# Turning LayerNorm's output by transposing DMAs of float16 halves instead of by TensorE

## The chip, the cores and the metric

The kernel runs on one core of one Trainium2 chip. A core has five engines that each run their own instructions in order: TensorE (PE, matrix products; its weight loads are shown apart as PEld), VectorE (DVE), ScalarE (ACT), GpSimd (POOL) and SyncE (SP), which here issues nearly all DMAs. The metric is the device time of one execution in microseconds (us), smaller is better, as the median over runs.

## The reference

The inputs are x of 2048 rows and 512 columns in float32, and the weights of an attention block and of a gated MLP. Cut to what matters:

```python
def _layernorm(x, axis=-1, eps=1e-5):
    m = jnp.mean(x, axis=axis, keepdims=True)
    v = jnp.var(x, axis=axis, keepdims=True)
    return (x - m) / jnp.sqrt(v + eps)

def attention(x, wqkv, wo):          # 32 heads of 16
    q, k, v = split(x @ wqkv)
    p = softmax(q @ k.T * 16 ** -0.5)
    return (p @ v) @ wo

def gated(x, w_in, w_sp, b_sp, w_out):   # w_in: 512 x 1376, w_sp: 2048 x 2048
    z = gelu(x @ w_in)
    z1, z2 = z[..., :688], layernorm(z[..., 688:])
    g = w_sp @ z2 + b_sp[:, None]
    return (z1 * g) @ w_out

h = x + attention(_layernorm(x), wqkv, wo)
out = h + gated(_layernorm(h), w_in, w_sp, b_sp, w_out)
```

## The kernel before

**Arithmetic.** Float32 products are made of float16 parts: an operand is split into `hi`, its float16 rounding, and `lo`, the float16 rounding of what is left. `mm3` (lines 107 to 109) makes three matmuls: hi by hi, hi by lo, lo by hi, all into one PSUM tile in float32.

**Stages.** The rows are worked in 16 blocks of 128. The prologue (0 to about 160 us) normalizes x block by block, turns each block so that the 512 columns lie on the partitions (four pieces of 128x128 side by side), and makes v, q and k of it; the attention stage (to about 1293 us) does the 32 heads and prepares the spatial products; the z stage (to about 1452 us) makes h, LN(h), gelu of its product with `w_in` and the LayerNorm of its second half, block by block; a last stage makes the spatial products and the output.

**How a block is turned.** The normalized block is float32 in SBUF. TensorE's `transpose` with an identity matrix turns one piece of 128x128 into PSUM, four to a block, into a tile `tp` (L424 in the prologue's `turn_only`, L1177 in the z stage's `turn`). Then ACT copies `tp` to a float16 tile (`hi`: L433, L98), and DVE subtracts that from `tp` for `lo` (L431, L104). The results are `xT` in the prologue and `hT` in the z stage.

**Order.** Around both places the order is written out by hand, under a manual schedule for all five engines: each engine does its instructions in the order of the program text, and waits where an operand or a buffer is not ready. A tile with `bufs=2` has two buffers; its third use waits until the first is read. SP issues the DMAs in text order too, and they are spread over eight lanes in turn: a DMA waits for the one eight places before it.

**The prologue's groups.** Blocks 4 to 15 go through a loop over g = 0, 1, 2, with a = 4g the blocks whose v is made by `proj(proj_v, ...)` and b = 4g + 4 the blocks that are normalized meanwhile. `stats` and `scales` (DVE) give mean and scale of four blocks at once, ending in `nb` (L401); `normal` (ACT, L412) normalizes one block in place (tile `xg`); `turn_x` turns blocks. `proj_qk` makes k and q of 512 rows, whose float16 parts `part` (ACT L458, DVE L461) go out to `k_scr` and `q_scr`; `kf` are two more copies by ACT of k for the maxima of the softmax (L472, L473), and v goes out to `v_scr`. PSUM has three tiles `acc` for these products, used in turn. In group 2 `load_wqk(1)` loads the next weights for q and k (`wg`, L345, on SP); `weigh_wqk(1)` takes their largest entries on DVE (`most`, L352) and spreads them on POOL (`each`, L356); `measure` is a small product of it on PE (`m`, L374), which stands in PE's order behind `proj_v(12)`.

**The z stage's loop.** Per block k, PE does `make_h` of block k + 2 (L747, 12 matmuls), then four products of 12 matmuls, `make_z`, of block k, with the transposes of block k + 1 between them. ACT does `split_o` of block k + 3 (tile `o`, L737, its `lo` on DVE L740), the four gelus of block k (L1192), `hT`, then `hn`, the normalized h of block k + 2 (L1271), and the normalization of z (L1214) with float16 copies of it (`b`, L1196). DVE does for each block: `o`, `hT`, the chain from `mv` (L758) to `nb` (L768) for LN(h) of block k + 2, in every second block a part `b` that was put off (L1197), the statistics of z (`zst`, L1265), the chain from `zmv` (L1211) to `nb`, then h itself (`xr`, L751) and its statistics. SP loads the attention's output `o` and the reciprocal row sums `rc` of block k + 5 (four DMAs each, L723 and L726) once `o`'s buffer is free; POOL multiplies the two (L731).

Of the kernel before, what the change touches and what calls it, by code (L numbers as in the profile page):

```python
# [59 lines left out]
def block_kernel(ctx: ExitStack, tc: tile.TileContext, x, wqkv, wo, w_in, w_sp4, b_sp, w_out, out):  # L60
# [208 lines left out]
    with ExitStack() as pre:  # L269
# [6 lines left out]

        xT = [pc.tile([P, DB, S], F16, name=f"xT{i}") for i in range(2)]
        wv = [pc.tile([P, DB, D], F16, name=f"wv{i}") for i in range(2)]
# [147 lines left out]
        def put_x(sb, *which):  # L426

            c = slice(sb * P, (sb + 1) * P)
            for i in which:
                if i:  # L430
                    nc.vector.tensor_sub(xT[1][:, :, c], tps[sb], xT[0][:, :, c])  # L431
                else:
                    nc.scalar.activation(xT[0][:, :, c], tps[sb], AF.Copy)  # L433

        def turn_x(*blocks):

            for sb in blocks:
                turn_only(sb)
                put_x(sb, 0, 1)
# [172 lines left out]
        for g in range(3):  # L612
            a, b = 4 * g, 4 * g + 4
            mv = moments(4)
            if g:
                proj(proj_v, a)
                turn_x(a + 2, a + 3)
                if g == 1:
# [6 lines left out]
                normal = scales(mv)  # L625
                normal(b, b + 1)
                proj(proj_v, a + 3)
# [14 lines left out]
            if g == 2:  # L642
                load_wqk(1)
            proj(proj_qk, 0, g, 0, then=lambda: turn_x(b, b + 1), at=1 if g else 2)
            if not g:
                load_x(12)
                load_x(13)
            normal(b + 2, b + 3)
        weigh_wqk(1)
        proj(proj_v, 12)  # L650
        turn_x(14, 15)
        load_wqk(2)
# [62 lines left out]
    h_rows = [0, 1, HB, HB + 1] + [sb + HB * i for sb in range(2, HB) for i in range(2)]  # L715
    os_, o2s, xrs, hns, hTs = {}, {}, {}, {}, {}

# [43 lines left out]
    def new_hn(sb):  # L761
        mv, rs = scale_h(sb)
        hns[sb] = e2.tile([P, D], F32, name="hn", bufs=3)
        nc.vector.tensor_scalar(hns[sb], xrs.pop(sb), mv[:, 0:1], rs, op0=ALU.subtract, op1=ALU.mult)

    def minus_mean(pool, mv, rs):
# [21 lines left out]
    with ExitStack() as at:  # L788
# [256 lines left out]
        for n in range(0, len(units), 2):  # L1045
# [94 lines left out]
            if n == 502:  # L1140
                new_hn(h_rows[0])
        weigh(*prev)
        take(*prev[:2], e2)
# [22 lines left out]
    with ExitStack() as mid:  # L1166
        m2 = mid.enter_context(tc.tile_pool(name="mid_2", bufs=2))
        zs, zst = {}, {}
        ps = mid.enter_context(tc.tile_pool(name="mid_ps", bufs=5, space=PSUM))
        pt = mid.enter_context(tc.tile_pool(name="mid_pt", bufs=2, space=PSUM))  # L1170

        def turn(sb):

            hn = hns.pop(sb)
            tp = pt.tile([P, DB, P], F32, name="tp")
            for d in range(DB):
                nc.tensor.transpose(tp[:, d, :], hn[:, d * P:(d + 1) * P], ident)  # L1177
            hTs[sb] = [m2.tile([P, DB, P], F16, name=f"hT{i}") for i in range(2)]
            split(hTs[sb][0], hTs[sb][1], tp, "act")

# [59 lines left out]
        with tc.manual_schedule(engines={E.PE, E.Activation, E.DVE, E.Pool, E.SP}):  # L1240
            asked.pop(0)()
            turn(row[0])
            new_hn(row[1])
            for k in range(NB):
                sb, new = row[k], row.get(k + 2)
# [6 lines left out]
                make_z(sb, 1, 0)  # L1252
                if k + 1 < NB and k != NB - 2:
                    turn(row[k + 1])
                if new is not None:
# [5 lines left out]
                if k == NB - 2:  # L1261
                    turn(row[k + 1])
                    put_off.pop()()
# [5 lines left out]
                if new is not None:  # L1269
                    hns[new] = e2.tile([P, D], F32, name="hn", bufs=3)  # L1270
                    nc.scalar.activation(hns[new], xrs.pop(new), AF.Identity, bias=nb, scale=rs)  # L1271
                if k == 1:
                    invert()
# [330 lines left out]
```

## Time and profile before

| | us |
|---|---|
| median of three runs | 1714.01 |
| lowest and highest run | 1713.07, 1714.47 |
| span of the profiled execution, first to last instruction | 1712.3 |
| PE busy in it | 1699.5 (99%) |
| DVE busy | 1452.5 (85%) |
| ACT busy | 1317.5 (77%) |
| POOL busy | 813.6 (48%) |

The profiled execution's own time is its span, 1712.3 us; the runs' times hold 1.7 us more, which lies around the first and the last instruction. In rows of a timeline the first number is the start in us, the second the duration in us, then the engine, the line, the operation, and the output tile, an arrow and the input tiles, then partitions by elements and types; "x2" means that several like instructions stand in one row, and brackets hold the idle time of the engine just before and what ended it. SPq is SP issuing a DMA: its length is the issue, not the transfer. In the chain of waits each piece is what the end of the program was waiting for, with a DMA piece as long as from issue to landing. Busy shares of PE are no measure of how full it is, since the ends of its matmuls are modelled.

### The profile page before, as it was taken

Reading aid. Unit: us, or ns where it says so; the run is one execution under the profiler, and the core shown is the slowest. Engines: PE = TensorE matmul, PEld = TensorE weight load, DVE = VectorE, ACT = ScalarE, POOL = GpSimd, SP = SyncE. Lnnn points to the kernel's source line nnn. Section 1 sums busy time; section 2 is a strip of 40 time slices with the busy share of each in tenths; the row PEclk is TensorE's granted clock in tenths of the full one; section 3 lists DMA queues with packets and bytes.
Section 4 is the critical chain, followed back from the end, with each engine's and each line's share of the span. In section 5 each row is a group of like instructions: output and inputs, shape, how many; then the busy total and the mean of one; then the engine's idle time right before and its main releaser. Section 6 shows DMA issues by size and latency. Waiting matters only on the chain.

```text
span 1712.3 us, 36689 instructions
## 1 busy us (share of the span) xinstructions
PE 1699.5 (99%) x13508; PEld 644.7 (38%) x13508; DVE 1452.5 (85%) x3051; ACT 1317.5 (77%) x2584; POOL 813.6 (48%) x1062
## 2 busy tenths in 40 slices
PE   9999999999999999999999999999999999999999
PEld 4533222222222222222222222222225666656665
DVE  7688999999999999999999999999936787543444
ACT  4334999999999999999999999999995545211111
POOL 1231867776673267687767776400002766300100
PEclk9999999999999999999999999999999999999999
DMA  5534332342221244344434444300114454664551
GB/s 185 167 94 144 103 89 68 101 94 82 81 68 25 56 118 117 104 144 125 130 113 124 132 140 130 80 13 19 37 39 124 140 173 140 233 234 156 198 217 44
DMA packets 189309, 196.03 MB, mean 114 GB/s; under 512 B 67496, under 2 KB 140008, under 8 KB 189128
## 3 DMA queue, kind: packets, MB, share of 16 engines
q1 hardware_dynamic: 186824, 188.04, 36.8%
q10 hardware_dynamic: 2304, 5.64, 0.8%
q8 instruction: 106, 1.74, 0.4%
q14 instruction: 75, 0.61, 0.1%
HBM read 122.10 MB, written 65.93 MB: 110 GB/s over the span
## 4 chain that ended last, share of the span: by engine, by line
PE 78%; DVE 12%; DMA 3%; POOL 2%; ACT 2%; SPq 2%; issue 1%; ACTq 0%; POOLq 0%; DVEq 0%
PE pv L830 26%; PE s L805 17%; PE m L223 9%; DVE mx L228 7%; PE acc L107 4%; PE g L108 4%; PE g L109 4%; PE g L107 4%; PE acc L109 4%; PE acc L108 4%; DMA rc<-r_scr 1%; DVE ab L237 1%; DVE og L840 1%; SPq L723 1%; DVE rs_t L124 1%
## 5 line engine op out<-in xcount | busy, mean ns | idle before, releaser
L814 ACT ACTIVATE pt<-s 128x512 f32<-128x512 f32 x1968 | 1006.2, 637 | 5.5 <-PE m L223 4.3
L228 DVE TENSOR_REDUCE mx<-m 128x1 f32<-128x512 f32 x1510 | 947.5, 682 | 11.7 <-PE m L223 2.9
L805 PE MATMUL s<-qst,kst 50*128 50x512 f16 x2048 | 604.2, 379 | 0.2
L830 PE MATMUL pv<-pt,vst 128*32 128x256 f32 (+1 forms) x6056 | 598.1, 466 | 4.1 <-DVE og L840 1.3
L223 PE MATMUL m<-kst,qst 48*128 48x512 f16 x1510 | 452.4, 381 | 0.0
L805 PEld LDWEIGHTS <-kst 50*128 50x128 f16 x2048 | 132.0, 94 | 352.1 <-issue 323.7
L830 PEld LDWEIGHTS pv<-pt,vst 128*32 128x32 f32 x6056 | 119.5, 108 | 290.7 <-issue 277.3
L223 PEld LDWEIGHTS <-qst 48*128 48x128 f16 x2048 | 159.2, 93 | 173.6 <-issue 124.2
L223 PE MATMUL m<-uvs,qst 48*128 48x512 f16 x504 | 190.5, 380 | 0.6 <-DVE mx L228 0.6
L245 POOL TENSOR_SCALAR nm<-nm 128x16 f32<-128x16 f32 x32 | 6.6, 206 | 358.8 <-DVE nm L242 358.8
L237 DVE CUSTOM_DVE_ANT_0 ab<-m,ab 128x512 f32<-128x512 f32 x252 | 170.5, 677 | 2.7 <-ACT ab L233 2.7
L233 ACT ACTIVATE ab<-m 128x512 f32<-128x512 f32 x252 | 157.3, 624 | 15.5 <-PE m L223 14.8
L1368 ACT ACTIVATE pr<-pr,up 128x304 f32<-128x304 f32 (+1 forms) x32 | 17.0, 574 | 109.2 <-DVE up L1322 109.2
L991 POOL TENSOR_TENSOR op<-raw,op 128x512 f16<-128x512 f32 x80 | 92.9, 1161 | 6.0
L914 POOL TENSOR_TENSOR raw<-raw 128x512 f32<-128x512 f32 (+1 forms) x84 | 83.3, 991 | 6.7
L919 POOL TENSOR_TENSOR acc_sp<-acc_sp,raw 128x512 f32<-128x512 f32 x63 | 80.4, 1277 | 4.5
L109 PE MATMUL acc<-wi,hT 128*128 128x344 f16 x256 | 79.1, 309 | 0.3 <-DVE hT L104 0.3
L107 PE MATMUL acc<-wi,hT 128*128 128x344 f16 x256 | 79.1, 309 | 0.0
L108 PE MATMUL acc<-wi,hT 128*128 128x344 f16 x256 | 79.1, 309 | 0.0
L1510 POOL TENSOR_TENSOR pr<-pr,z 128x344 f32<-128x344 f32 x8 | 7.3, 914 | 145.9 <-DMA whole<-squares 108.3
L911 POOL TENSOR_SCALAR raw<-raw 128x512 f32<-128x512 f32 (+1 forms) x88 | 52.3, 594 | 19.7 <-DMA raw<-in_wqkv 12.4
L1509 DVE TENSOR_TENSOR pr<-g,v 128x344 f32<-128x344 f32 x8 | 4.1, 517 | 66.6 <-PE g L109 63.5
(247 smaller groups left out, 2292.9 us busy)
## 6 DMA issues: line engine op xcount, KB each, us to landing
raw<-in_w_sp SPq DMA_DIRECT2D x128, 256.0 KB
s_scr<-op SPq DMA_DIRECT2D x64, 256.0 KB
op<-s_scr SPq DMA_DIRECT2D x32, 512.0 KB
a_scr<-op SPq DMA_DIRECT2D x48, 256.0 KB
op<-a_scr SPq DMA_DIRECT2D x24, 512.0 KB
o_scr<-og SPq DMA_DIRECT2D x64, 128.0 KB
qst<-q_scr SPq DMA_DIRECT2D x192, 32.0 KB
kst<-k_scr SPq DMA_DIRECT2D x48, 128.0 KB
```

Of the source, the lines that this page charges most:

```text
L107: nc.tensor.matmul(ps, lh, rh, start=first, stop=False, **kw)
L108: nc.tensor.matmul(ps, lh, rl, start=False, stop=False, **kw)
L109: nc.tensor.matmul(ps, ll, rh, start=False, stop=last, **kw)
L223: nc.tensor.matmul(acc, q[r, p, c], keys[r, p], start=True, stop=True)
L228: nc.vector.reduce_max(at(t, e if t else e - 1), acc, axis=AX.X)
L233: nc.scalar.activation(ab[0], acc, AF.Abs)
L237: nc.vector.tensor_tensor_reduce(ab[0], acc, ab[0], 0.5, LOW, ALU.add, ALU.max, at(0, 0))
L805: nc.tensor.matmul(s, kst[hg % 2][r, p, kb * P:(kb + 1) * P], qst[hg * NQ + qb][r, p, :], start=True, stop=True)
L814: nc.scalar.activation(pts[p, kb][:, t, :], s, AF.Exp, scale=scales_[hg // 2])
L830: nc.tensor.matmul(pv[0][32 * j:32 * j + 32, a:b], vst[hg % 2][:, c:c + 32], pts[j % 2, kb][:, j // 2, a:b], start=kb == 0, stop=kb == NB - 1,
L914: pool.tensor_mul(got[0] if n else acc, got[0], got[0])
L991: chores.append((lambda: pool.tensor_sub(t[0][:, 1], of(), t[0][:, 0]), TT))
```

## The change

Two of the places where TensorE turned a block now use a DMA that transposes 2-byte elements on its way from SBUF to SBUF. The order of halving and turning is swapped: the block is split into its float16 halves first, side by side in one tile of 128 x 1024, and one DMA turns all eight pieces of it.

- Prologue, blocks 8 to 15: `split_x` makes `hi` by an ACT copy and `lo` by a POOL subtraction in a tile `xp` (two buffers), and SP issues the transposing DMA into `xT`, which is now one tile for both halves. Each block is split right behind its normalization. Blocks 0 to 7 are turned by TensorE as before.
- z stage, all 16 blocks: `halve_h` makes `hi` by an ACT copy (DVE for the first block), `turn_h` makes `lo` by a DVE subtraction in a tile `hp` (two buffers), and SP issues the transposing DMA into `hT`. The two PSUM tiles that `turn` used go to the pool of products, which has 7 in place of 5. A block is turned two blocks ahead of its use, and not one.

```diff
@@ -274,7 +274,8 @@
         pt = pre.enter_context(tc.tile_pool(name="pre_pt", bufs=2, space=PSUM))
         more[3] = more[4] = lambda: pt.tile([P, 512], F32, name="tp")
 
-        xT = [pc.tile([P, DB, S], F16, name=f"xT{i}") for i in range(2)]
+        xTs = pc.tile([P, 2, DB, S], F16, name="xT")
+        xT = [xTs[:, i] for i in range(2)]
         wv = [pc.tile([P, DB, D], F16, name=f"wv{i}") for i in range(2)]
         w4 = wqkv.rearrange("(a p) c -> p a c", p=P)
         xs, xns, wqk, wvs = {}, {}, {}, {}
@@ -431,6 +432,17 @@
                     nc.vector.tensor_sub(xT[1][:, :, c], tps[sb], xT[0][:, :, c])
                 else:
                     nc.scalar.activation(xT[0][:, :, c], tps[sb], AF.Copy)
+
+        def split_x(*blocks):
+
+            for sb in blocks:
+                xn = xns.pop(sb)
+                xp = p2.tile([P, 2, D], F16, name="xp")
+                nc.scalar.activation(xp[:, 0], xn, AF.Copy)
+                nc.gpsimd.tensor_sub(xp[:, 1], xn, xp[:, 0])
+                nc.sync.dma_start_transpose(
+                    xTs[:, :, :, sb * P:(sb + 1) * P].rearrange("p i d s -> p (i d) s"),
+                    xp.rearrange("p i c -> p (i c)"))
 
         def turn_x(*blocks):
 
@@ -614,7 +626,8 @@
             mv = moments(4)
             if g:
                 proj(proj_v, a)
-                turn_x(a + 2, a + 3)
+                if g == 1:
+                    turn_x(a + 2, a + 3)
                 if g == 1:
                     load_x(14)
                     load_x(15)
@@ -623,7 +636,9 @@
                 stats(mv, b + 2, b + 3)
                 proj(proj_v, a + 2)
                 normal = scales(mv)
-                normal(b, b + 1)
+                for sb in range(b, b + 4):
+                    normal(sb)
+                    split_x(sb)
                 proj(proj_v, a + 3)
             else:
                 proj(proj_v, 2, on_act=True)
@@ -641,14 +656,15 @@
                 normal(b + 1)
             if g == 2:
                 load_wqk(1)
-            proj(proj_qk, 0, g, 0, then=lambda: turn_x(b, b + 1), at=1 if g else 2)
-            if not g:
+            if g:
+                proj(proj_qk, 0, g, 0)
+            else:
+                proj(proj_qk, 0, g, 0, then=lambda: turn_x(b, b + 1), at=2)
                 load_x(12)
                 load_x(13)
-            normal(b + 2, b + 3)
+                normal(b + 2, b + 3)
         weigh_wqk(1)
         proj(proj_v, 12)
-        turn_x(14, 15)
         load_wqk(2)
         load_wqk(3)
         measures.pop(0)()
@@ -713,7 +729,7 @@
     wi4 = w_in.rearrange("(a p) c -> p a c", p=P)
 
     h_rows = [0, 1, HB, HB + 1] + [sb + HB * i for sb in range(2, HB) for i in range(2)]
-    os_, o2s, xrs, hns, hTs = {}, {}, {}, {}, {}
+    os_, o2s, xrs, hns, hps, hTs = {}, {}, {}, {}, {}, {}
 
     def load_o(sb):
 
@@ -762,6 +778,22 @@
         mv, rs = scale_h(sb)
         hns[sb] = e2.tile([P, D], F32, name="hn", bufs=3)
         nc.vector.tensor_scalar(hns[sb], xrs.pop(sb), mv[:, 0:1], rs, op0=ALU.subtract, op1=ALU.mult)
+
+    def halve_h(sb, on_act=True):
+
+        hps[sb] = e2.tile([P, 2, D], F16, name="hp")
+        if on_act:
+            nc.scalar.activation(hps[sb][:, 0], hns[sb], AF.Copy)
+        else:
+            nc.vector.tensor_copy(hps[sb][:, 0], hns[sb])
+
+    def turn_h(sb):
+
+        hp = hps.pop(sb)
+        nc.vector.tensor_sub(hp[:, 1], hns.pop(sb), hp[:, 0])
+        t = e2.tile([P, 2 * DB, P], F16, name="hT")
+        nc.sync.dma_start_transpose(t, hp.rearrange("p i c -> p (i c)"))
+        hTs[sb] = [t[:, :DB], t[:, DB:]]
 
     def minus_mean(pool, mv, rs):
         nb = pool.tile([P, 1], F32, name="nb")
@@ -1139,6 +1171,9 @@
                 steps_h.append(make_h(h_rows[1], later[0].tile([P, 512], F32, name="h")))
             if n == 502:
                 new_hn(h_rows[0])
+            if n == 504:
+                halve_h(h_rows[0], False)
+                turn_h(h_rows[0])
         weigh(*prev)
         take(*prev[:2], e2)
         asked.append(load_o(h_rows[4]))
@@ -1166,17 +1201,7 @@
     with ExitStack() as mid:
         m2 = mid.enter_context(tc.tile_pool(name="mid_2", bufs=2))
         zs, zst = {}, {}
-        ps = mid.enter_context(tc.tile_pool(name="mid_ps", bufs=5, space=PSUM))
-        pt = mid.enter_context(tc.tile_pool(name="mid_pt", bufs=2, space=PSUM))
-
-        def turn(sb):
-
-            hn = hns.pop(sb)
-            tp = pt.tile([P, DB, P], F32, name="tp")
-            for d in range(DB):
-                nc.tensor.transpose(tp[:, d, :], hn[:, d * P:(d + 1) * P], ident)
-            hTs[sb] = [m2.tile([P, DB, P], F16, name=f"hT{i}") for i in range(2)]
-            split(hTs[sb][0], hTs[sb][1], tp, "act")
+        ps = mid.enter_context(tc.tile_pool(name="mid_ps", bufs=7, space=PSUM))
 
         def new_z(sb):
             zs[sb] = [m2.tile([P, FH], F32, name=f"z{i}", bufs=1 + 3 * i) for i in range(2)]
@@ -1239,8 +1264,9 @@
         row = dict(enumerate(h_rows))
         with tc.manual_schedule(engines={E.PE, E.Activation, E.DVE, E.Pool, E.SP}):
             asked.pop(0)()
-            turn(row[0])
             new_hn(row[1])
+            halve_h(row[1])
+            turn_h(row[1])
             for k in range(NB):
                 sb, new = row[k], row.get(k + 2)
                 if new is not None:
@@ -1250,8 +1276,6 @@
                     split_o(row[k + 3])
                 new_z(sb)
                 make_z(sb, 1, 0)
-                if k + 1 < NB and k != NB - 2:
-                    turn(row[k + 1])
                 if new is not None:
                     mv, rs = scale_h(new)
                     nb = minus_mean(e2, mv, rs)
@@ -1259,7 +1283,6 @@
                     subs.pop()(nc.vector)
                 make_z(sb, 1, 1)
                 if k == NB - 2:
-                    turn(row[k + 1])
                     put_off.pop()()
                 for c in range(2):
                     nc.vector.bn_stats(zst[sb][:, c, :], zs[sb][1][:, c * FC:(c + 1) * FC])
@@ -1269,6 +1292,8 @@
                 if new is not None:
                     hns[new] = e2.tile([P, D], F32, name="hn", bufs=3)
                     nc.scalar.activation(hns[new], xrs.pop(new), AF.Identity, bias=nb, scale=rs)
+                    halve_h(new)
+                    turn_h(new)
                 if k == 1:
                     invert()
                 if k >= NB - 8:
```

The lines behind the changed functions move down: SP's v_scr L493 becomes L505, the transposing DMA is L443 in the prologue.

SP's order in the prologue, groups 1 and 2, before (`v_scr` is a block of v that goes out, `qst` and `wg` are loads, `wg` that of the next weights):

```order
L493 DMA v_scr<-v 128x512 x3
L194 DMA qst<-q_scr 16x2x512 x6
L493 DMA v_scr<-v 128x512
L464 DMA k_scr<-part 128x2x512
L481 DMA uv_scr<-part 64x2x512 x2
L464 DMA q_scr<-part 128x2x512
L493 DMA v_scr<-v 128x512 x4
L345 DMA wg<-in_wqkv 128x4x128 x2
L464 DMA k_scr<-part 128x2x512
```

The same place with the change:

```order
L505 DMA v_scr<-v 128x512 x2
L443 DMA_TRANSPOSE xT<-xp 128x8x128 x4
L505 DMA v_scr<-v 128x512
L194 DMA qst<-q_scr 16x2x512 x6
L505 DMA v_scr<-v 128x512
L476 DMA k_scr<-part 128x2x512
L493 DMA uv_scr<-part 64x2x512 x2
L476 DMA q_scr<-part 128x2x512
L505 DMA v_scr<-v 128x512 x2
L443 DMA_TRANSPOSE xT<-xp 128x8x128 x4
L505 DMA v_scr<-v 128x512 x2
L346 DMA wg<-in_wqkv 128x4x128 x2
```

Each group's four transposing DMAs stand among the blocks of v, and the second four stand ahead of `wg`.

ACT's order in group 1 with the change (`xg` is `normal`, `xp` the copy of `split_x`; the names in brackets are what it waits for, where DMAHW7 and DMAHW0 are the lanes of the first and second transposing DMA of the group):

```order
L413 ACTIVATE xg<-xg,nb_612,rs_r_600 128x512 [waits DMAHW0_49,DVE_49,Pool_49]
L441 ACTIVATE xp<-xg 128x512 [waits Activation_49]
L413 ACTIVATE xg<-xg,nb_612,rs_r_600 128x512 [waits DMAHW1_49,Pool_49]
L441 ACTIVATE xp<-xg 128x512 [waits Activation_49]
L413 ACTIVATE xg<-xg,nb_612,rs_r_600 128x512 [waits DMAHW2_49]
L441 ACTIVATE xp<-xg 128x512 [waits DMAHW7_49,Activation_49,Pool_49]
L413 ACTIVATE xg<-xg,nb_612,rs_r_600 128x512 [waits DMAHW3_49]
L441 ACTIVATE xp<-xg 128x512 [waits DMAHW0_49,Activation_49,Pool_49]
L470 ACTIVATE part<-acc 128x512 [waits PE_49]
L484 ACTIVATE kf_695<-acc 64x512 [waits DVE_49]
```

Before, `part` stood between the second and the third `xg`, and `kf` behind the fourth; now all four normalizations and copies come first, and the third and fourth copy wait for a landing.

DVE's order in the z stage, where the LayerNorm of h ends and that of z begins, with the change:

```order
L126 TENSOR_SCALAR rs_u<-rs_t_22527,rs_u 128x1
L800 TENSOR_SCALAR nb<-rs_u,mv 128x1
L1222 TENSOR_TENSOR b_1_20647<-z_22362,b_0_20646 128x344
L1288 BN_STATS zst<-z_22505 128x6 x2
L793 TENSOR_TENSOR hp<-hn,hp 128x512
L1236 BN_AGGR zmv<-zst 128x2
L114 TENSOR_SCALAR rs_v_22596<-zmv 128x1
```

Before, `zmv` followed `zst` directly, and the subtraction for `hT` stood between `o` and `mv`; now that place is empty and the subtraction for `hp`, which needs ACT's `hn` and its copy, stands between `zst` and `zmv`.

## The prediction

> **What bounds the kernel now.** The page's head and its first part say that TensorE (PE) is the engine to look at over the whole span:
>
> ```profile
> span 1712.3 us, 36689 instructions
> PE 1699.5 (99%) x13508; PEld 644.7 (38%) x13508; DVE 1452.5 (85%) x3051; ACT 1317.5 (77%) x2584; POOL 813.6 (48%) x1062
> ```
>
> A share over the span does not tell what a removed PE instruction is worth in one stage, so next comes the chain of waits in the prologue, around the changed blocks (start, length, piece):
>
> ```profile
> by line: PE acc L108 29.5%; PE acc L109 29.5%; PE acc L107 28.8%; PE tp L424 11.6%; PE m L374 1.4%
> ...
> 46.21 0.87 PE tp L424 x8
> 50.97 0.87 PE tp L424 x8
> 63.50 0.87 PE tp L424 x8
> 68.26 0.87 PE tp L424 x8
> ```
>
> Nothing but PE stands on this chain between 40 and 70 us: there, each us of PE that goes is a us, if nothing new is late. Eight blocks are turned in four pairs of 0.87 us, so 3.5 us can go; one block is 0.44 us, and the z stage's 16 blocks are 7.0 us. Ceiling: 10.5 us, or 1703.5.
>
> The z stage is another matter. The chain at its beginning, where blocks follow each other at PE's own pace:
>
> ```profile
> 1304.63 2.59 PE acc L747 x12
> 1314.66 2.59 PE acc L747 x12
> ```
>
> That is 10.03 us a block, 20.06 a pair; without the transposes PE would need 9.59 a block, 19.2 a pair. Later in the stage the timelines of ACT and DVE over two blocks show another pace (in brackets the idle time before):
>
> ```profile
> 1374.24 0.72 ACT L737 ACTIVATE o<-o,fig 128x512 f16<-128x512 f32 x1
> 1379.03 0.81 ACT L1271 ACTIVATE hn<-xr,nb,rs_u 128x512 f32<-128x512 f32 x1 [1.83 <-DVE nb L768]
> 1384.18 0.72 ACT L737 ACTIVATE o<-o,fig 128x512 f16<-128x512 f32 x1
> 1393.30 0.96 ACT L1214 ACTIVATE z<-z,nb,rs_u 128x688 f32<-128x688 f32 x1 [3.52 <-DVE nb L768]
> 1394.68 0.72 ACT L737 ACTIVATE o<-o,fig 128x512 f16<-128x512 f32 x1
> ...
> 1375.91 0.69 DVE L104 TENSOR_TENSOR hT<-tp,hT 128x512 f16<-128x512 f32 x1
> 1376.52 0.17 DVE L758 BATCH_NORM_AGGREGATE mv<-st 128x2 f32<-128x6 f32 x1
> 1378.91 0.93 DVE L1265 BATCH_NORM_STATS2 zst<-z 128x6 f32<-128x344 f32 x2
> 1379.87 0.21 DVE L1211 BATCH_NORM_AGGREGATE zmv<-zst 128x2 f32<-128x12 f32 x1
> ...
> 1385.85 0.69 DVE L104 TENSOR_TENSOR hT<-tp,hT 128x512 f16<-128x512 f32 x1 [0.17 <-ACT hT L98]
> 1386.46 0.17 DVE L758 BATCH_NORM_AGGREGATE mv<-st 128x2 f32<-128x6 f32 x1
> 1388.85 1.02 DVE L1197 TENSOR_TENSOR b<-z,b 128x344 f16<-128x344 f32 x1
> 1389.79 0.92 DVE L1265 BATCH_NORM_STATS2 zst<-z 128x6 f32<-128x344 f32 x2
> 1390.75 0.21 DVE L1211 BATCH_NORM_AGGREGATE zmv<-zst 128x2 f32<-128x12 f32 x1
> ```
>
> From o to o the two blocks take 9.94 and 10.50 us, 20.44 for the pair, more than PE needs. ACT stands idle before `hn` and before L1214, each time for DVE's `nb`; DVE then waits for ACT's `o`. It is a loop of these two: o, DVE's two LayerNorm chains one after the other, L1214, o. PE waits for `o` inside it, and 0.44 us less on PE is worth nothing here as long as the loop is longer than PE's work.
>
> **The change, part by part: prologue.** Removed: 3.5 us of PE, and per block an ACT copy and a DVE subtraction out of PSUM. Added, per block: an ACT copy to `xp`, a POOL subtraction, a transposing DMA on SP. In ACT's new order the copy of the third block of a group waits for the landing of the first (two `xp` buffers), the fourth for the second, and `part` and `kf` queue behind. On SP, the loads `wg` of the next weights, issued at 62.30 before, now stand behind four transposing DMAs and two `v_scr`. Rows for it:
>
> ```profile
> 42.92 1.52 ACT L412 ACTIVATE xg<-xg,nb,rs_r 128x512 f32<-128x512 f32 x2 [7.68 <-issue]
> 45.01 0.60 ACT L458 ACTIVATE part<-acc 128x512 f16<-128x512 f32 x1 [0.56 <-ACT xg L412]
> 52.35 1.16 POOL L479 TENSOR_TENSOR part<-uv,part 128x512 f16<-128x512 f32 x1
> 48.22 0.38 PE L107 MATMUL acc<-wv,xT 128*128 128x512 f16 x1
> 48.35 0.53 SPq L493 DMA_DIRECT2D v_scr<-v  x1
> 59.96 0.16 DVE L401 SCALAR_TENSOR_TENSOR nb<-mv,rs_r 128x4 f32<-128x4 f32 x1
> 62.30 0.96 SPq L345 DMA_DIRECT2D wg<-in_wqkv  x2
> 66.17 1.28 DVE L352 TENSOR_REDUCE most<-wg 128x1 f32<-128x512 f32 x2 [0.28 <-DMA wg<-in_wqkv]
> 68.97 0.60 PE L374 MATMUL m<-each,every 128*128 128x256 f32 x2
> ```
>
> A row block's normalization is 0.8 us on ACT, its copy 0.6 (as `part`), its subtraction 1.16 (same shape and types). No row shows a transposing DMA. Call T its time from SP's issue to landing. The chain has these DMA pieces, by length:
>
> ```profile
> 743.34 1.94 DMA sums<-o_scr
> 870.34 4.17 DMA raw<-in_w_sp
> 1322.88 7.05 DMA o<-o_scr
> 1369.03 5.19 DMA rc<-r_scr
> ```
>
> Bounds: 1.94 with 0.4 of issue, so 2.3, and 7.05 with 0.6, so 7.7. `raw` moves 256 KB, as one `xp` does: I take 4.17 + 0.4, T = 4.5. The Trainium skill ("DMA: Bandwidth & Descriptors", the row on DMA_TRANSPOSE's effective bandwidth in its table) gives 261 GB/s, by which 256 KB would take an estimated 1.0 us; the sum by it would be the low end or a little under.
>
> Blocks 8 to 11, T = 4.5: normalized at 43.7, copied 44.3, subtracted 45.5, landed 50.0. PE, with one pair removed, wants block 8 at 48.22 - 0.87 = 47.35: 2.65 us late. On ACT block 10's copy ends at 50.6, block 11's normalization at 51.4, its copy 52.0; `part` and two `kf`, taken at 0.6 each like it, end at 53.8. The PSUM tile that these free is wanted by PE's second next product, at 50.0 + 2.6: 1.2 more. PE is 3.85 late.
>
> Blocks 12 to 15: `nb` ends at 60.12 - 1.74 (two pairs removed) + 3.85 = 62.2. Block 12 is subtracted at 64.8 and lands at 69.3; block 14's copy waits for that and ends at 69.9; block 15 is normalized at 70.7, copied 71.3, subtracted 72.5. Its issue (0.4) and two `v_scr` (0.53 each) put `wg` at 74.0 instead of 62.30. From `wg`'s issue to PE's `m` it was 6.67 us, and all of it was on DMA, DVE and POOL: `m` at 80.6. Before: 68.97. **Prologue: +11.7 us**, the removed 3.5 included; behind `m` PE is the chain again and has no stall to give it back from. The same steps give +7.2 at T = 2.3, +18.0 at T = 7.7, and +4.7 even at T = 0: four blocks take ACT 5.6 us where `wg` had no slack.
>
> **z stage.** Removed from DVE: L104, after which `mv` starts 0.70 earlier in the first block of a pair and 0.76 in the second. Added to DVE: a subtraction s that stands between `zst` and `zmv`, and waits for ACT's `hn` and its new copy. First block: `hn` ends at about 1379.15 (0.70 earlier than before), the copy 0.65 later, so `zmv` starts at 1379.85 + s, against 1379.87: 9.92 + s. Second: `b` and `zst` end after the copy, `zmv` starts 0.76 earlier plus s: 9.74 + s. Pair: 19.66 + 2s. The nearest rows for s are the same shape and types out of SBUF, in one group:
>
> ```profile
> L334 DVE TENSOR_TENSOR wv<-wg,wv x2: 678/885/1092, 15.0 to 16.0; 128x512 f16<-128x512 f32 x2
> ```
>
> One took 0.68, one 1.09; DVE's L1197, as long as 1.02 for 344 columns while POOL worked beside it, would be 1.5 for 512. I take s = 1.0: 21.66, or +1.22 a pair. The loop's stretch is some 11 blocks, 5.5 pairs: +6.7. The four or so blocks before it are PE's and gain 0.44 each, -1.8. **z stage: +4.9 us** (s = 0.68: +0.58 a pair, +1.4 in all; s = 1.36: +1.94 a pair, +10.7 if the early blocks gain nothing).
>
> On SP the transposing DMA stands ahead of the loads of a later row, and waits for that subtraction:
>
> ```profile
> 1365.27 2.48 SPq L723 DMA_DIRECT2D o<-o_scr  x4
> 1375.82 2.48 SPq L723 DMA_DIRECT2D o<-o_scr  x4
> 1377.98 1.27 POOL L731 TENSOR_TENSOR o<-o,rc 128x512 f32<-128x512 f32 x1
> ```
>
> The loads of 1365.27 are multiplied at 1377.98 and split at 1384.18; the last of them lands at 1374.2 by the chain (1369.03 + 5.19). The subtraction ends at 1380.85, and with 0.6 of issue the loads start at 1381.45, 5.6 later; they land at 1379.9, counted on before's times, and are multiplied by 1381.2: 3.0 us spare, so this wait costs nothing as long as SP's issue stays under some 3 us.
>
> **Sum.** 1712.3 + 11.7 + 4.9 = 1728.9 of span. The runs' median, 1714.0, lies 1.7 above the span: **1730.6 us**. Low: +7.2 + 1.4, 1722.6. High: +18.0 + 10.7, 1742.7.
>
> **Rivals.**
> - Slow transposing DMAs, T at twice the slowest `rc` (10.4). The prologue's steps give +23.4. In the z stage each DMA waits for the eighth before it: the last `rc` issues 4.4 us behind the transposing DMA, so it waits 6 us, uses up the 3.0 spare and is 3.0 late in two blocks: 5.5 times that less 1.8, +15. Total 1752. For it: the packets of 256 bytes that such a turn needs; against: no row. The Trainium skill ("VectorE: DVE Perf Modes", The three transpose paths) has 1309 ns for one 128x128 by DMA against 390 on TensorE, and says to use TensorE where PSUM will do; eight pieces one after the other are an estimated 10.5 us, this rival. The trace's transposes of PE, 0.22 us each when pipelined, are cheaper than the page's.
> - The z stage gains: if s fits the time in which DVE waits and PE runs ahead with two more PSUM tiles, -7.0; with the prologue's least, +4.7, the time is 1711.7, no difference. Against: DVE's rows above follow one another, and s is 0.68 at the least.
> - The prologue hidden: if `wg` were early enough, -3.5 + 4.9: 1715.4. Against: `most` stood 0.28 us idle for `wg` already.
> - Faster: both hidden, PE's 10.5 us all gained, 1703.5. It decides if T is under 1.85 and `wg` has 12 us of slack; the rows deny the second.
>
> **How the numbers follow.** Forecast 0.70, slow DMAs 0.15, z gains 0.06, prologue hidden 0.04, faster 0.05. A measurement of this kernel tells 0.2%, 3.4 us. Faster 0.05, same 0.10, slower 0.85. The range goes from 1716, over the hidden prologue's edge, to 1752, the slow rival's centre.
>
> **What would show it.** Right: PE idle before block 8's first product and before `m` L374, the latter 8 to 18 us late with `wg` issued near 74; pairs of z blocks of 21 to 22 us with DVE's subtraction near 1.0. Wrong: `m` before 74, or pairs under 20.4. If T is under 2 us, 1722 is too high still; if SP's issue itself takes over 3 us, the z loads bite and the time passes 1743.

## The result, and the profile after

The changed kernel takes 1729.64 us (median of four runs, 1729.27 to 1731.33), the kernel before took 1713.54 beside it (1712.59 to 1714.47). The ratio is 1.0098, with a 95% interval of 1.0085 to 1.011: 16.1 us slower. The forecast was 1730.6, in a range of 1716 to 1752.

The page of the changed kernel, its head and first row:

```profile
span 1728.1 us, 36528 instructions
PE 1695.0 (98%) x13412; PEld 633.6 (37%) x13412; DVE 1446.1 (84%) x3044; ACT 1319.8 (76%) x2583; POOL 824.5 (48%) x1070
```

PE is busy 4.5 us less than before and the span is 15.8 us longer: work was removed from PE, and waits took more than its place. Where they lie is told by two landmarks, which don't depend on how busy shares are modelled: the first product of the attention stage (`s`) and the last of its closing products (`pv`). From the answers by source line (least, median and longest duration in ns, then the first and last start in us), before:

```profile
L805 PE MATMUL s<-qst,kst x2048: 372/376/387, 160.2 to 1290.3; 50*128 50x512 f16 x187
L830 PE MATMUL pv<-pt,vst x6056: 379/403/618, 164.8 to 1293.1; 128*32 128x256 f32 x126, 128*32 128x512 f32 x70
```

and after:

```profile
L837 PE MATMUL s<-qst,kst x2048: 372/376/387, 174.3 to 1304.2; 50*128 50x512 f16 x187
L862 PE MATMUL pv<-pt,vst x6056: 379/403/618, 178.8 to 1306.9; 128*32 128x256 f32 x126, 128*32 128x512 f32 x70
```

The attention stage starts 14.1 us later (174.3 against 160.2) and ends 13.8 later; the rest of the span, 15.8 - 13.8 = 2.0 us, is put down to the z stage, the only part behind it that was changed. So the prologue made 14 of the 16 us. In seven traces with an unchanged prologue (the kernel before and six of the runs below) the attention stage starts between 159.6 and 160.8, so a start is known to about 0.6 us.

In the prologue, SP's timeline (SPq is the issue alone):

```profile
46.10 8.02 SPq L443 DMA_TRANSPOSE xT<-xp  x4
64.98 7.94 SPq L443 DMA_TRANSPOSE xT<-xp  x4
73.02 1.02 SPq L505 DMA_DIRECT2D v_scr<-v  x2
74.13 1.04 SPq L346 DMA_DIRECT2D wg<-in_wqkv  x2
```

and PE's rows that follow idle time:

```profile
49.51 0.39 PE L107 MATMUL acc<-wv,xT 128*128 128x512 f16 x1 [1.55 <-DMA xT<-xp]
54.09 0.38 PE L107 MATMUL acc<-wv,xT 128*128 128x512 f16 x1 [1.83 <-ACT kf L485]
68.32 0.39 PE L107 MATMUL acc<-wv,xT 128*128 128x512 f16 x1 [1.11 <-DMA xT<-xp]
80.46 1.22 PE L375 MATMUL m<-each,every 128*128 128x256 f32 x2 [9.38 <-POOL each L357]
```

The waits stand where the prediction's steps put them: block 8's landing, the PSUM tile behind `kf`, block 12's landing (which it times without calling it a wait of PE), and `m`, which waits 9.38 us for the weights that left SP at 74.13 in place of 62.30. The chain of waits has the time of one transposing DMA, from the start of its issue to its landing, and what PE does behind the long wait:

```profile
46.10 3.36 DMA xT<-xp
...
64.98 3.29 DMA xT<-xp
...
80.46 1.22 PE m L375 x2
81.69 0.43 PE acc L107
...
85.10 0.43 PE acc L109
85.53 0.22 PE acc L107
```

The nine products behind `m` take 0.43 us each, those after them 0.22. The windows of the same trace, cut at the wait (start and end, length, the busy time of PE, PEld, DVE, ACT and POOL, and in the last three columns the granted clock, the mean busy share of the DMA engines and GB/s):

```profile
71.00:75.00 4.00, 0.08 (x1) 0.00 (x0) 0.68 (x1) 0.39 (x1) 0.65 (x1) 1.00 0.93 207
75.00:80.40 5.40, 0.00 (x0) 0.00 (x0) 1.88 (x3) 0.00 (x0) 0.71 (x2) 0.51 0.64 186
80.40:85.40 5.00, 4.94 (x12) 2.10 (x13) 1.70 (x6) 0.00 (x0) 2.41 (x4) 0.50 0.77 213
85.40:90.00 4.60, 4.60 (x23) 2.12 (x22) 1.32 (x2) 0.60 (x1) 2.50 (x4) 1.00 0.63 214
```

PE stands idle from 71.08. Its granted clock is halved some 4 us into the wait, and stays so for 5 us after work has come back.

In the z stage, DVE's subtraction and the part `b` in the middle of the stage, and ACT's `o` over several blocks (timelines):

```profile
1374.79 0.69 DVE L793 TENSOR_TENSOR hp<-hn,hp 128x512 f16<-128x512 f32 x1 [0.70 <-ACT hp L786]
1383.61 0.51 DVE L1222 TENSOR_TENSOR b<-z,b 128x344 f16<-128x344 f32 x1
...
1335.82 0.72 ACT L753 ACTIVATE o<-o,fig 128x512 f16<-128x512 f32 x1
1347.24 0.72 ACT L753 ACTIVATE o<-o,fig 128x512 f16<-128x512 f32 x1 [0.94 <-POOL o L747]
1358.88 0.72 ACT L753 ACTIVATE o<-o,fig 128x512 f16<-128x512 f32 x1 [0.74 <-POOL o L747]
1369.30 0.72 ACT L753 ACTIVATE o<-o,fig 128x512 f16<-128x512 f32 x1
1389.77 0.72 ACT L753 ACTIVATE o<-o,fig 128x512 f16<-128x512 f32 x1
1410.13 0.72 ACT L753 ACTIVATE o<-o,fig 128x512 f16<-128x512 f32 x1
```

and of the kernel before, the block of 1369.30:

```profile
1353.81 0.72 ACT L737 ACTIVATE o<-o,fig 128x512 f16<-128x512 f32 x1
```

From 1369.30 a pair of blocks takes 20.47 and 20.36 us, as before the change (20.44): 1369.30 lies 15.5 us behind 1353.81, and 1410.13 lies 15.5 behind the 1394.68 of its block before. Of the z stage's loss 1.7 us (15.5 - 13.8) had come about by then. Ahead of 1369.30 two blocks take 11.4 and 11.6, and at their ends ACT stands idle for POOL's product of `o` and `rc`.

### The profile page after: what moved, and what is told of

Read it like the earlier page. It is cut to its first block, busy times and chain, and to the rows that moved or that the text cites. A ratio compares the mean times of both kernels' runs of the same rounds, so it can differ in the third digit from the quotient of the medians.

```text
span 1728.1 us, 36528 instructions
## 1 busy us (share of the span) xinstructions
PE 1695.0 (98%) x13412; PEld 633.6 (37%) x13412; DVE 1446.1 (84%) x3044; ACT 1319.8 (76%) x2583; POOL 824.5 (48%) x1070
## 4 chain that ended last, share of the span: by engine, by line
PE 74%; DVE 13%; DMA 3%; issue 3%; POOL 2%; ACT 2%; SPq 2%; POOLq 0%; ACTq 0%; DVEq 0%
PE pv L862 25%; PE s L837 17%; PE m L223 9%; DVE mx L228 7%; PE g L107 4%; PE g L108 4%; PE g L109 4%; PE acc L107 3%; PE acc L109 3%; PE acc L108 3%; DVE ab L237 1%; DVE og L872 1%; DVE rs_t L124 1%; DMA hT<-hp 1%; DMA rc<-r_scr 1%
## 5 line engine op out<-in xcount | busy, mean ns | idle before, releaser
L747 POOL TENSOR_TENSOR o<-o,rc 128x512 f32<-128x512 f32 x16 | 20.4, 1274 | 98.6 <-DMA rc<-r_scr 50.0
```

## The experiments

The theory was: the prologue loses because the weights for `m` stand on SP behind four transposing DMAs that themselves wait for ACT's copies, and because PE's clock is halved in that wait; the z stage loses little, through loads that stand behind the transposing DMA. The rivals: the turned blocks themselves are what PE waits for; the half speed has another cause; DVE's loop is the z stage's loss.

**Each part alone.** The first run has the prologue's edits and the z stage as before, the second the reverse.

> Only the prologue's part of the change; the z stage turns by TensorE as before. In the changed kernel's trace the attention stage starts 14.1 us later than before (174.3 against 160.2) and the end lies 15.8 us later, so the theory (nearly all of the loss is made in the prologue) expects 14 us over the time before, about 1727.5. The rival, by the prediction's own split, is +11.7 from the prologue, 1725.2, and the rest from the z stage.

> Only the z stage's part of the change; the prologue as before. The theory expects +1.5 to +2.0 us over the time before, about 1715.3: pairs of blocks near 20.4 us as before, the subtraction on DVE 0.69 instead of 1.0, and a few waits for late loads early in the stage. The rival, the prediction's term of +4.9, would be 1718.4.

Measured: 1726.45 (ratio to before 1.0077, 1.006 to 1.0094) and 1717.02 (1.002, 1.0011 to 1.003), against 1713.15 beside them: +13.3 and +3.9. The attention stage of the first starts at 174.1, that of the second at 160.3. The prologue's part is confirmed; the z stage's part costs more by itself than the 2.0 us that the changed kernel's trace shows for it, and its runs spread from 1715.0 to 1718.2; its profiled span is 3.0 over that of before. Its size lies between 2 and 5 us.

**The weights first.**

```diff
                 normal = scales(mv)
+                if g == 2:
+                    load_wqk(1)
                 for sb in range(b, b + 4):
...
-            if g == 2:
-                load_wqk(1)
```

> The changed kernel with the load of the next weights (wg) issued ahead of the second four transposing DMAs. If PE's long wait before the small product m is for these weights behind the transposing DMAs, as predicted, the loads leave near 63 instead of 74.1, m moves from 80.5 to about 74.5 (DVE's maximum still stands behind a part that waits for ACT's copies), and the time falls by 6.0 to 8.5 us, to 1721 to 1723.6; the larger figure if PE's stretch of half speed behind m goes with the shorter wait. If the wait is for the turned blocks themselves, nothing changes.

Measured: 1722.01 (1.0054, 1.0037 to 1.0071), 7.6 us under the changed kernel. SP and PE, from the timelines of this run:

```profile
62.57 1.66 SPq L346 DMA_DIRECT2D wg<-in_wqkv  x2
64.32 8.98 SPq L443 DMA_TRANSPOSE xT<-xp  x4
...
68.70 0.39 PE L107 MATMUL acc<-wv,xT 128*128 128x512 f16 x1 [2.30 <-DMA xT<-xp]
74.12 0.70 PE L375 MATMUL m<-each,every 128*128 128x256 f32 x2 [0.97 <-POOL each L357]
```

`m` moved from 80.46 to 74.12, near the 74.5 that was expected, and the attention stage's start from 174.3 to 165.5. The transposing DMAs now stand behind the weights, and PE's wait for block 12 grew from 1.11 to 2.30. The half speed did not go: the products from 69.70 to 72.26 stand 0.43 apart, behind a wait of 2.30. The window of this stretch has the granted clock at 0.52, with less on the DMA engines (0.36) than in the changed kernel's stretch (0.77):

```profile
69.50:73.00 3.50, 3.50 (x10) 1.06 (x7) 1.63 (x3) 2.19 (x4) 2.27 (x2) 0.52 0.36 68
```

**The wait filled.**

```diff
-            tp = bank(1)[:, :2 * P].rearrange("p (i c) -> p i c", i=2)
+            full = bank(1)
+            for _ in range(42 if b == 1 else 0):
+                nc.tensor.matmul(full, idle[:, :P], idle, start=True, stop=True)
+            tp = full[:, :2 * P].rearrange("p (i c) -> p i c", i=2)
```

> The changed kernel with 42 empty products (9.1 us of PE) put into PE's wait of 9.4 us before m; nothing else is moved. Behind that wait the trace has ten products at 0.43 us in place of 0.22 and a granted clock of 0.55 in the stretch from 80.4 to 86. If the idle time causes it, the stretch goes and the time falls by 2.5 us, to about 1727. If the half speed has another cause (the DMAs beside it), nothing changes.

Measured: 1727.64 (1.0084, 1.0067 to 1.01), 2.0 us under the changed kernel; the attention stage starts at 171.9, 2.4 earlier. The windows of this run have, for the stretch that the expectation names:

```profile
80.40:86.00 5.60, 5.50 (x25) 2.65 (x26) 2.46 (x7) 0.00 (x0) 3.47 (x6) 1.00 0.77 214
```

The granted clock is 1.00 there in place of 0.55, with the DMA engines busy all the same (0.77): PE's idle time causes the half speed. 171.9 is 11.7 over the start before, the prediction's term; that the tenths agree means nothing, since a start is known to 0.6 us. The half speed, 2.0 us by the runs and 2.4 by the traces, is what the term lacked.

**More buffers.** The weights first, and:

```diff
-                xp = p2.tile([P, 2, D], F16, name="xp")
+                xp = p2.tile([P, 2, D], F16, name="xp", bufs=4)
...
             proj(proj_qk, 0, g, 1)
+            if g == 2:
+                weigh_wqk(1)
...
-        weigh_wqk(1)
         proj(proj_v, 12)
```

> The changed kernel with the weights' load first, as in the run before, and besides four buffers for xp in place of two and the largest entries of the weights taken on DVE and POOL ahead of the parts that wait for ACT. ACT's third and fourth copy no longer wait for a landing (2.65 and 2.53 us in the changed kernel), so kf frees PE's PSUM tile in time (1.8 us), and the subtractions end near 67.4. By the measured 3.4 us from issue to landing PE still waits 1.5 us for block 8 and 1.5 for block 12, and m comes near 70, so the attention stage should start 1 to 2 us later than before in place of 5.3 in the run with the weights' load first, and the time be 1716 to 1718. If the buffers don't matter, the time stays at 1722.

Measured: 1716.85 (1.0021, 1.0011 to 1.0031), as expected; the 3.6 us over the time before agree with the z stage's part alone (3.9). The attention stage starts at 160.3, where it started before the change: of the 14.0 us down from 174.3 the weights' place on SP made 8.8 (to 165.5), and the two further edits of this run the other 5.2. How these share it, the copies' wait for a landing against the place of the weights' largest entries on DVE, was not tested apart. PE's waits from 20 to 160 us are now one row (us in all, times, longest):

```profile
PE acc L107 <- DMA xT<-xp: 3.1, 2, 1.6
```

So with this queueing gone, 3.1 us of waits for the first block of each group eat the 3.5 us that PE saves.

**z stage: the loads first.** The z stage's part alone, with `load_o` ahead of `turn_h` on SP:

```diff
                     nc.scalar.activation(hns[new], ...)
+                    if k + 5 < NB:
+                        asked.append(load_o(row[k + 5]))
                     halve_h(new)
                     turn_h(new)
...
-                    if k + 5 < NB:
-                        asked.append(load_o(row[k + 5]))
```

> The z stage's part of the change alone, with a later row's loads of o and rc issued ahead of the transposing DMA instead of behind it. If the rest of the z stage's loss comes from POOL's product waiting for these loads (ACT stood idle for it before o in three blocks, 1.9 us), the time falls by 1.5 to 2.5 us against the z stage's part alone (1717.0), to about 1715. If the loss is DVE's loop, it stays at 1717.

Measured: 1714.84 (1.0011, 1.0002 to 1.002), 2.2 us under the z stage's part alone. The place of these loads on SP is more than half of that part's loss; what is left, 1.6 us, is clear of noise, if barely. By the traces of the two runs PE's waits for `o` fell from 7.3 us to 1.9, while those for `hT`, whose DMA now stands behind the loads, rose from 0.8 to 4.4: part of the wait moved.

**z stage: the subtraction late.** The same, and:

```diff
                     halve_h(new)
-                    turn_h(new)
+                    if k == NB - 3:
+                        turn_h(new)
...
             nb = minus_mean(m2, mv, rs)
+            for new in late:      # late: the block new, where there is one
+                turn_h(new)
             nc.scalar.activation(z[1], z[1], AF.Identity, bias=nb, scale=rs)
```

> As the run with the loads first, and DVE's subtraction for hp moved from between zst and zmv to behind the nb of z, where DVE later waits 0.8 to 1.2 us for o. Then the loop loses the subtraction (0.69) and the wait for ACT's copy ahead of it (0.27 to 0.70): the two blocks of a pair would take 9.24 each by DVE's rows, under PE's own 9.6, so PE is the limit. 11 blocks from 10.22 to 9.6 are -6.8 us, the earlier ones -0.4 each: 5 to 8 us under the time before, 1705 to 1708. If the loop isn't DVE's chain, it stays near 1715.

Measured: 1716.55 (1.0022, 1.0013 to 1.0031): a miss. Rows of PE in this run:

```profile
1364.89 2.75 PE L747 MATMUL acc<-wo,o 128*128 128x512 f16 x12
1374.48 2.75 PE L747 MATMUL acc<-wo,o 128*128 128x512 f16 x12
1384.07 2.75 PE L747 MATMUL acc<-wo,o 128*128 128x512 f16 x12
...
1409.03 0.32 PE L107 MATMUL acc<-wi,hT 128*128 128x344 f16 x1 [2.16 <-DMA hT<-hp]
```

In the middle of the stage the pace is 9.59 us, PE's own: DVE's loop was the bound, as the expectation had it, and is no longer. But the turn is now late for PE, which waits for `hT` in eight blocks, up to 2.2 us and 8.1 in all; the transposing DMA of the last of these rows was issued at 1400.74 and had landed at 1409.0, 8 us.

**The turn between the loads.** The same, with the loads of `rc` and `xr` (`rest_o`, the second half of `load_o`) and the 512 KB loads for the last stage (`ask`) behind the transposing DMA:

```diff
-                        asked.append(load_o(row[k + 5]))
+                        first_o(row[k + 5])
...
-                if k >= NB - 8:
-                    ask()
...
                 def meanwhile(k=k):
+                    if k + 5 < NB:
+                        asked.append(rest_o(row[k + 5]))
...
                     gate_z(sb, meanwhile, () if new is None else (new,))
+                if k >= NB - 8:
+                    ask()
```

> As the late subtraction (z stage alone), but on SP the transposing DMA stands behind the four loads of o alone: the loads of rc and xr, and the 512 KB loads of the last stage, follow it. In the late subtraction's trace PE keeps its own pace of 9.59 us a block wherever it doesn't wait for hT, and waits for hT in 9 blocks, 8 us in all; the landing came up to 8 us after the issue, behind those loads. If the turn is late because it stands behind them in SP's queue, most of the 8 us goes: 4 to 7 us under that run, 1709 to 1712. If the DMA itself is as slow under load wherever it stands, the time stays at 1716.

Measured: 1716.81 (1.0023, 1.0014 to 1.0032), a miss in the total. PE keeps 9.6 us a block from 1313 to 1390 without a wait for `hT`, so the order on SP was what made the turn late in those blocks. From there, where the 512 KB loads begin, blocks take 11.5, 12.6 and 13.4 (PE's first products of `o` at 1390.05, 1401.54, 1414.10 and 1427.54), with PE waiting for `o` in three of them (5.1 us) and for `hT` in one (1.5). The windows of this run, and then of the kernel before:

```profile
1293.00:1390.00 97.00, 96.10 (x600) 58.51 (x599) 79.48 (x252) 53.35 (x89) 60.63 (x67) 1.00 0.70 164
1390.00:1455.00 65.00, 55.11 (x342) 32.35 (x342) 45.38 (x154) 32.09 (x57) 38.18 (x47) 1.00 0.72 173
```

```profile
1293.00:1390.00 97.00, 96.64 (x611) 59.54 (x606) 76.73 (x241) 48.94 (x85) 54.35 (x62) 1.00 0.48 140
1390.00:1455.00 65.00, 64.63 (x419) 40.72 (x418) 50.87 (x169) 34.05 (x61) 41.58 (x50) 1.00 0.47 153
```

With the transposing DMAs the mean busy share of the DMA engines is 0.70 in place of 0.48, for 24 GB/s more. But the mean share doesn't tell the good stretch (0.70) from the bad one (0.72). SP's timeline does, with the issue of the four loads of `o` and of the transposing DMA, ahead of 1390 and behind it:

```profile
1383.59 2.48 SPq L727 DMA_DIRECT2D o<-o_scr  x4
1388.17 1.27 SPq L787 DMA_TRANSPOSE hT<-hp  x1
1406.66 4.63 SPq L727 DMA_DIRECT2D o<-o_scr  x4
1412.29 2.66 SPq L787 DMA_TRANSPOSE hT<-hp  x1
```

`rc` stands behind these on SP and POOL's product needs it, so a longer issue ahead of it can make `o` late. Ahead of 1390 the same order cost nothing.

**The first block of each group by PE.** The prologue's part with more buffers, the z stage as before, and blocks 8 and 12 turned by TensorE:

```diff
                     normal(sb)
-                    split_x(sb)
+                    if sb > b:
+                        split_x(sb)
...
-                proj(proj_qk, 0, g, 0)
+                proj(proj_qk, 0, g, 0, then=lambda: turn_x(b))
```

> The prologue's part alone (z stage as before), as in the run with more buffers, but with the first block of each group turned by TensorE again: blocks 9 to 11 and 13 to 15 by DMA. The two waits of 1.5 and 1.6 us for blocks 8 and 12 go, at the price of 2 x 0.44 on PE. The attention stage should start at 160.3 - 3.1 + 0.9 = 158.1, and the time be 2 us under that of before, 1711. If the waits only move to blocks 9 and 13, the attention stage starts at 160 and the time is that of before.

Measured: 1713.30 (1.0001, 0.9992 to 1.001), no difference from before, and the attention stage starts at 160.4. The waits moved, though not to blocks 9 and 13: PE waits 0.9 us for ACT's `hi` of the block that it turned and 1.2 for DVE's `lo`, since ACT now makes the copies of the other three blocks first. That this is the reason was read from ACT's order and not tested.

**Both.** That prologue with the z stage of the turn between the loads.

> The two runs beside this one put together: the prologue with the first block of each group by TensorE, and the z stage with the late subtraction and the turn between the loads. The gains should add, since an engine's order in the one stage leaves the other alone: 1709 to 1712 less 2, so 1707 to 1710, against 1713.2 before.

Measured: 1718.13 (1.003, 1.0019 to 1.0041). A miss: neither part had gained, and nor does the sum, which is 4.8 us over the time before, against 3.4 and 0 for the parts.

**The large loads spread, or half of the blocks by PE.** Two edits of the turn between the loads, to tell what costs from 1390 on: the 512 KB loads in every second block of the whole stage; or the last six blocks turned by TensorE, as before (`turn` and its PSUM tiles are back for these).

```diff
-                if k >= NB - 8:
+                if k % 2 == 0:
                     ask()
```

```diff
                 make_z(sb, 1, 0)
+                if LAST < k + 1 < NB and k != NB - 2:
+                    turn(row[k + 1])
...
-                    halve_h(new)
+                    if k + 2 <= LAST:      # LAST = 9
+                        halve_h(new)
```

> As the turn between the loads (z stage alone), with the eight loads of 512 KB for the last stage spread over the whole z stage (every second block) instead of the last eight blocks. In that run PE kept 9.59 us a block up to 1390 and lost it where these loads begin (waits of 1.4 to 2.2 us for ACT's o), while the mean busy share of the DMA engines was 0.70 and 0.72 against 0.48 and 0.47 before. If the coincidence of the loads with the transposing DMAs is what costs, the late waits shrink and the time falls by 3 to 5 us, to 1712 to 1714. If it is the sum of what the DMA engines carry in the stage, the waits move to other blocks and the time stays at 1716 to 1717.

> As the turn between the loads (z stage alone, the 512 KB loads in the last eight blocks as before), but only the first ten blocks are turned by DMA and the last six by TensorE again. The DMA engines are then free of transposing DMAs while the 512 KB loads run. If they are the cause of the late loss, PE keeps 9.59 us a block in the first half (4.4 us gained there) and the pace of before, 10.2, in the second: 1709 to 1710.5, faster than before. If the late loss has another cause, the time is 1714 or more.

Measured: 1722.18 (1.0049, 1.0036 to 1.0063) and 1711.93 (0.9992, 0.9983 to 1.0001). Both miss their ranges. Spreading the loads made it 5.4 us worse, which neither branch of the expectation had: PE now waits for `o` 0.6, 1.5 and 1.7 us in blocks ahead of 1370 as well. Taking the transposing DMAs away from the late blocks gave 4.9 back, less than the 6 to 8 expected: PE keeps 9.59 up to 1381, then 10.03 from 1404 on, with two longer blocks between. So in these runs the cost appears where 512 KB loads and transposing DMAs meet. Whether it lies in what the DMA engines carry, or in the longer issues on SP that push `rc` back, these runs don't tell apart, since both edits change the two at once. The second run has the lowest time of all, but its interval includes the time of before; no version was found that is clearly faster.

## Why the prediction was right

**The total** was right (1730.6 against 1729.64), and so were the sign and the mechanism of its largest term, the weights that stand on SP behind the transposing DMAs. That the total is right to 1 us is luck: the prologue's term was 2.4 too low and the z stage's 2.9 too high, and inside each of them errors offset one another. By its own steps:

- "Nothing but PE stands on this chain": not contradicted. With the queueing gone (more buffers) the start should lie at 160.2 - 3.5 + 3.1 = 159.8, and lies at 160.3, within the 0.6 us. No run shows a gain in the prologue that is larger than this.
- The prologue's path: right in place, and in size partly by luck. `wg` left SP at 74.13 (predicted 74.0) and `m` stood at 80.46 (80.6). Inside, T was 3.36 and not 4.5, while the issue was 1.25 us (median 1.26 of eight) and not 0.4; PE's first two waits were 1.55 and 1.83 and not 2.65 and 1.2; and `nb` of group 1 was 0.44 later than before, from a later start of PE's work (10.92 against 10.46 for its first weighing product) that lies ahead of the change. These offset one another.
- "+11.7": measured +14.1, of which `m` has 11.5 (80.46 - 68.97). The step that failed is "behind `m` PE is the chain again": it is, at half speed for 5 us. The filled wait shows that, with 11.7.
- s: mis-sized, 0.69 instead of 1.0 in thirteen of sixteen subtractions, and in all of the pairs above; the other three, at 1320.93, 1352.81 and 1364.44, took 0.92 to 1.03. Besides, `b` on DVE fell from 1.02 to 0.51, which no step had.
- The loop: its form was right, its loss 0 and not 1.22 a pair. With s = 0.69 the prediction's 19.66 + 2s is 21.04, and measured are 20.47 and 20.36. Taking the whole 0.51 of `b` off it gives 20.53, but DVE then waits 0.27 us for ACT's copy, so `b` is worth 0.24. The rest is in the starts of the rows: the subtraction holds up the next by 0.61 and not 0.69, twice, and `mv` starts 0.80 earlier in the block without `b` and not 0.70. That comes to 20.54.
- "z stage: +4.9": 2.0, and by two errors. The loop's +6.7 was 0. The early blocks' -1.8 was +1.7: PE has its pace of 9.59 in some of them (its products of `o` at 1309.20 and 1318.79, and at 1328.68 and 1338.27), but waits 1.73 us for DVE ahead of the first, where it waited 0.22 before, and the block with the late loads takes 11.64.
- "3.0 us spare, so this wait costs nothing": right in the loop's stretch, where ACT waits for POOL's product once, for 0.25 us, and wrong in the two blocks ahead of it, where it waits 0.94 and 0.74 (1347.24 and 1358.88). The condition, an issue of the transposing DMA under some 3 us, held: none in the stage took over 2.63. But the loads for 1358.88, which left at 1344.10 behind an issue of 1.92, took 5.08 us to issue where the step had 2.48. The loads first gave 2.2 us back, which shows that their place on SP costs; why their issue grew stays open, with the load on the DMA engines as the reading at hand.
- The signs. Of those for "right", PE's idle time before block 8 and `m`, `m` 11.5 us late and `wg` near 74 came; pairs of 21 to 22 us with the subtraction near 1.0 did not, and one pair, 20.36, lies under the 20.4 that was named as a sign of "wrong". The total was right with a z stage that was not.
- The rivals. T at 10.4 is refuted for the prologue (3.36); in the z stage of the late subtraction a landing came 8 us after the issue. "Faster" asked for T under 1.85 and for slack of `wg`, and had neither. "The prologue hidden" has its condition in the run with more buffers, where `wg` is early: 1716.85 against its 1715.4, but the prologue then gives 0 and not -3.5, since PE waits for the landings. In "the z stage gains", the pace of 9.59 came, for seven blocks on end, in the turn between the loads, but no run has gained the stage as a whole.
- A slip that nothing hangs on: a transpose on PE takes 0.11 us in the trace (0.87 for eight), not 0.22.

## What to carry to other kernels

Work that is taken off the bounding engine is worth its time only if everything it now queues with keeps its place: here most of the loss came from a load that had nothing to do with the turn, and stood behind it on SP. Cost a new DMA three times: its landing, its issue on the queue, and what it takes of the DMA engines while other loads run. Where a change makes PE wait, add the half speed behind the wait: here it followed waits of 2.3 and 9.4 us.

## What the runs showed of the hardware

- A transposing DMA of 256 KB in float16 from SBUF to SBUF takes SP 1.25 us to issue and 3.3 to 3.4 us to land in the changed kernel's prologue; four one after the other were issued in 5.49 us (more buffers). In the z stage an issue took up to 2.63 us, and 4.31 in the turn between the loads. The queue rows of the page, before and after:

```profile
q1 hardware_dynamic: 186824, 188.04, 36.8%
```

```profile
q1 hardware_dynamic: 212168, 194.33, 40.3%
```

The 24 DMAs add (0.403 x 1728.1 - 0.368 x 1712.3) = 66 us of all sixteen engines, with 1056 packets each. If all other packets took as long as before, which isn't shown, that is 2.8 us for each DMA, an estimate of some 95 GB/s while it runs. The Trainium skill's figure of 261 GB/s ("DMA: Bandwidth & Descriptors", the table's row on DMA_TRANSPOSE) is not reached in this kernel by that estimate, and the estimate from its 1309 ns for a 128x128 piece ("VectorE: DVE Perf Modes", The three transpose paths) is three times too long for eight pieces in one DMA: 3.36 us, or 0.42 a piece. The Trainium skill's advice to turn by TensorE where PSUM will do ("VectorE: DVE Perf Modes", Rules for kernel authors) is borne out as far as these runs go: none that turns by DMA is clearly faster than the kernel before.

- PE's granted clock was halved 4 us into a wait of 9.4, and also behind a wait of 2.3, some 0.8 us after work had come back (the weights first); waits of 1.55 and 1.83 in the changed kernel did not do it. The Trainium skill ("TensorE: Matmul & The Clock Gate", Part 1) has half rate after an idle window of about 3.4 us, with windows that run freely; the first wait agrees, the second is shorter than its window. The first cost 2.4 us.

- DVE's `b` (344 columns) took 1.02 us in six of seven cases before and 0.51 in five of seven with the change. In these POOL is at work beside it, before on a subtraction and after mostly on a cast. But the seventh before, and one of the five after, took 0.51 and 0.52 beside subtractions of POOL. So POOL at work beside it doesn't settle the time; what does was not tested.
